# Loading the first q and k in halves of consecutive rows, with a new queue order, in an attention and MLP-mixer kernel

## The chip, the cores and the metric

The kernel runs on one core of one Trainium2 chip. The time of a run is the device time of that core in microseconds (us). Every run is listed with the mean granted clock of TensorE; a run is in the fast state when it is within 1.5% of the fastest of the same kernel.

## The reference, cut to what matters

```python
# q, k, v: (4, 8, 768, 64) float32; n_sink = 4, window = 128
scores = q @ k.T / 8                                  # per batch and head
keep   = (key < 4) | (0 <= query - key < 128)         # four sink keys and a window
a      = softmax(where(keep, scores, -1e9))
x      = (a @ v) in (4, 768, 512)
h  = relu(x^T @ w_tok1) @ w_tok2                      # mixes the 768 rows
u  = x + h^T
out = u + relu(u @ w_ch1) @ w_ch2                     # mixes the 512 channels
```

## The kernel before

The kernel works in eight groups of four heads. Two groups make a batch; after them TensorE runs the token products and then the channel products of that batch. Each operation is an object with its dependencies, and a small scheduler in the program orders them before anything is emitted; a list `FIRST` fixes the order of the start by hand. The first stage of a group is: load q and k, cast to bf16, transpose on VectorE in 32x32 blocks, scores.

```python
GH, Q = 4, 32                      # heads of a group; partitions of one head
PIECES = (2, 1, 1, 1, 1, 1, 1, 1)  # parts in which q and k of a group are loaded
...
C = PIECES[g]; R = S // Q // C     # S = 768: 24 rows of every partition, 12 in a half
for n, (w, c) in enumerate([(w, c) for c in range(C) for w in "qk"]):
    # partition (h, i) holds rows 24*i to 24*i + 23 of head h; part c is 12 of every 24 rows
    src = heads(q if w == "q" else k, g).rearrange("h (i r) d -> (h i) r d", i=Q)[:, ts(c, R)]
    ...
    nc.sync.dma_start(out=raws[w][:, ts(c, R)], in_=src)
...
# the transpose of part c fills 12 of every 24 columns of qT or kT
nc.vector.transpose(G.T[w].rearrange("p s x -> p (s x)").bitcast(UINT32)
                    .rearrange("p (i r) -> p r i", i=Q)[:, r], G.bf[w][:, r].bitcast(UINT32))
...
deps = G.dt["q"] + G.dt["k"]       # a score tile needs all transposes of its group
```

So a score tile of 128 consecutive keys needs both halves. A load of group 0 is one instruction for 128 partitions with 3072 contiguous bytes each, 393,216 bytes. The weights of the token products are issued by GpSimd's queue after v of group 0 has landed.

The softmax here doesn't subtract the row's maximum and nothing guards it: scores larger than these inputs give would overflow.

## Time and profile before

| | before |
|---|---|
| median of 3 runs, us | 216.26 (216.06 to 216.56) |
| span of the profiled run, us | 215.0 |
| mean granted clock of TensorE | 1.00 |
| TensorE busy | 204.2 us, 95% |
| first score matmuls | 10.42 us |
| first channel matmuls, in the chain | 31.30 us |

The prediction below shows the chain and the page. The view of busy time by stretch: the stretch, its length, the busy time of the five engines with the number of instructions, the granted clock, the busy share of the 16 DMA engines, and the GB/s that they moved.

```profile
core 0: us, PE busy (x) PEld busy (x) DVE busy (x) ACT busy (x) POOL busy (x), PEclk, DMA share, GB/s
5.00:10.00 5.00, 4.80 (x23) 1.96 (x20) 3.83 (x4) 2.66 (x4) 3.53 (x9) 1.00 0.98 355
15.00:20.00 5.00, 5.00 (x78) 2.86 (x74) 4.67 (x10) 4.49 (x6) 3.11 (x4) 1.00 1.11 173
```

The timeline (start, length, engine, line, operation, output and input, and in brackets how long the engine had been idle and what ended it): the casts of the two first halves.

```profile
4.29 0.84 ACT L235 ACTIVATE qb<-raw_q 128x768 bf16<-128x768 f32 x1 [0.16 <-DMA raw_q<-in_q_dram]
5.22 0.84 ACT L235 ACTIVATE kb<-raw_k 128x768 bf16<-128x768 f32 x1
```

### The profile page before, as it was taken

How to read it: one execution, taken by the hardware profiler on the slowest of the kernel's cores; microseconds unless marked ns; L12 is line 12 of the kernel's file. 1: busy time of each engine (PE TensorE's matmuls, PEld its weight loads, DVE VectorE, ACT ScalarE, POOL GpSimd, SP SyncE). 2: the span in 40 equal slices, each digit the busy share in tenths (PEclk: the TensorE clock that was granted, in tenths of full speed). 3: DMA queues.
4: the chain of work that ended last, by engine and by line, in shares of the span. 5: the costliest groups of instructions: out<-in, count | busy, mean ns of one | idle time of the engine just before them, and what ended most of it. 6: DMA issues, size and time to landing. Idle time of an engine off the chain costs nothing.

```text
span 215.0 us, 4175 instructions
## 1 busy us (share of the span) xinstructions
PE 204.2 (95%) x1764; PEld 115.8 (54%) x1764; DVE 128.2 (60%) x224; ACT 108.3 (50%) x178; POOL 33.3 (15%) x54
## 2 busy tenths in 40 slices
PE   7899999999689999979999999999999999999993
PEld 2336766554246655556655544667555545655552
DVE  4778941689899999988998912787531122001121
ACT  8489456534837233989627520696453302743300
POOL 7648810002262200211000000000000000000000
PEclk9999999999999999999999999999999999999999
DMA  6999999999999993860001012200001122001122
GB/s 193 366 226 169 204 198 203 206 208 233 219 223 236 250 196 85 161 110 0 3 0 49 3 49 107 92 0 3 0 3 49 49 97 98 3 2 49 49 98 101
DMA packets 36244, 24.68 MB, mean 115 GB/s; under 512 B 26112, under 2 KB 30976, under 8 KB 36224
## 3 DMA queue, kind: packets, MB, share of 16 engines
q1 hardware_dynamic: 29184, 15.73, 28.9%
q0 software_dynamic: 7040, 8.67, 24.1%
q8 instruction: 14, 0.23, 0.4%
q14 instruction: 6, 0.05, 0.1%
HBM read 26.77 MB, written 6.29 MB: 154 GB/s over the span
## 4 chain that ended last, share of the span: by engine, by line
PE 85%; DVE 7%; ACT 3%; DMA 3%; issue 1%; SPq 0%; ACTq 0%
PE ps_w L687 29%; PE ps_v L665 28%; PE ps_s L455 6%; PE ps_h L580 5%; PE ps_u L632 5%; DVE pT L483 4%; PE ps_o L531 3%; DMA raw_q<-in_q_dram 3%; PE ps_o L528 2%; PE ps_o L536 2%; PE ps_ut L642 2%; ACT pT L472 2%; DVE x_b L552 1%; PE ps_s L448 1%; PE ps_k L509 1%
## 5 line engine op out<-in xcount | busy, mean ns | idle before, releaser
L665 PE MATMUL ps_v<-uT,w_ch 128*128 128x384 bf16 x384 | 67.9, 326 | 0.0
L239 ACT ACTIVATE v<-ps_v 128x384 bf16<-128x384 f32 x89 | 43.5, 493 | 48.5 <-PE ps_v L665 37.3
L687 PE MATMUL ps_w<-w_ch,v 128*128 128x512 bf16 (+1 forms) x300 | 66.1, 371 | 0.0
L472 ACT ACTIVATE pT<-ps_s 128x1024 bf16<-128x1024 f32 (+1 forms) x48 | 43.7, 954 | 13.8 <-PE ps_s L455 9.4
L665 PEld LDWEIGHTS <-w_ch 128*128 128x128 bf16 x384 | 36.5, 98 | 25.3 <-DVE x_b L552 0.4
L697 DVE TENSOR_TENSOR o<-ps_w,u_sb 128x512 f32<-128x512 f32 (+1 forms) x25 | 16.7, 669 | 55.8 <-PE ps_w L687 55.8
L687 PEld LDWEIGHTS <-v 128*128 128x128 bf16 x300 | 28.9, 98 | 29.6 <-issue 0.2
L483 DVE TENSOR_TENSOR pT<-pT,mrest 128x1536 bf16<-128x1536 bf16 (+2 forms) x21 | 23.1, 1098 | 1.5 <-ACT pT L472 1.5
L637 DVE TENSOR_TENSOR u_sb<-ps_u,x_b 128x512 bf16<-128x512 f32 x24 | 15.2, 684 | 10.1 <-PE ps_u L632 10.1
L552 DVE TENSOR_TENSOR x_b<-ps_o,rc 128x256 bf16<-128x256 f32 (+1 forms) x45 | 19.9, 442 | 1.6
L455 PE MATMUL ps_s<-qT,kT 32*128 32x256 bf16 (+1 forms) x384 | 18.2, 264 | 1.6 <-ACT pT L472 1.0
L403 DVE STREAM_TRANSPOSE qT<-qb 128x768 uint32<-128x768 uint32 (+1 forms) x9 | 16.8, 1869 | 4.1 <-ACT qb L235 1.8
L531 PE MATMUL ps_o<-va,pT 128*128 128x65 bf16 x192 | 16.3, 194 | 1.7 <-DVE o L697 1.4
L403 DVE STREAM_TRANSPOSE kT<-kb 128x768 uint32<-128x768 uint32 (+1 forms) x9 | 16.9, 1874 | 0.4 <-POOL kb L234 0.4
L234 POOL CAST va<-raw_v 128x1536 bf16<-128x1536 f32 x7 | 10.5, 1493 | 42.2 <-DMA raw_v<-in_v_dram 27.2
L455 PEld LDWEIGHTS <-kT 32*128 32x128 bf16 x384 | 9.8, 92 | 11.9 <-issue 8.3
L531 PEld LDWEIGHTS <-pT 128*128 128x128 bf16 x192 | 13.4, 98 | 3.7 <-DVE o L697 1.7
L536 PE MATMUL ps_o<-va,pT 128*128 128x65 bf16 x160 | 14.8, 193 | 0.0
L632 PE MATMUL ps_u<-h,w_tok 128*128 128x512 bf16 x48 | 12.6, 378 | 0.6 <-ACT uT L235 0.5
L580 PE MATMUL ps_h<-x_b,w_tok 128*128 128x256 bf16 x96 | 12.2, 273 | 0.0
L536 PEld LDWEIGHTS <-pT 128*128 128x128 bf16 x160 | 11.3, 98 | 0.8 <-issue 0.3
L235 ACT ACTIVATE uT<-ps_ut 128x512 bf16<-128x512 bf16 (+1 forms) x14 | 7.8, 566 | 7.5 <-PE ps_ut L642 7.3
(63 smaller groups left out, 135.8 us busy)
## 6 DMA issues: line engine op xcount, KB each, us to landing
out_dram<-o SPq DMA_DIRECT2D x23, 256.0 KB, 2.0
raw_v<-in_v_dram SPq DMA_DIRECT2D x7, 768.0 KB, 12.3
qb<-in_q_dram POOLq DMA_DIRECT2D x6, 384.0 KB, 8.3
kb<-in_k_dram POOLq DMA_DIRECT2D x6, 384.0 KB, 12.2
w_ch<-in_moe_w_ch_dram POOLq DMA_DIRECT2D x4, 384.0 KB, 9.5
w_ch<-in_moe_w_ch_dram POOLq DMA_DIRECT2D x1, 1024.0 KB, 15.2
raw_q<-in_q_dram SPq DMA_DIRECT2D x2, 384.0 KB, 4.5
raw_k<-in_k_dram SPq DMA_DIRECT2D x2, 384.0 KB, 5.1
```

The source lines that it names most:

```text
L239: nc.scalar.activation(o, i, AF.Relu)
L403: nc.vector.transpose(G.T[w].rearrange("p s x -> p (s x)").bitcast(UINT32).rearrange("p (i r) -> p r i", i=Q)[:, r], G.bf[w][:, r].bitcast ...
L455: nc.tensor.matmul(bank[h][:, at:at + w], G.T["k"][r, ts(kt, P), db], G.T["q"][r, ds(kt * P, w), db], start=not pem and db == 0, stop=db = ...
L472: nc.scalar.activation(o, i, AF.Exp, scale=scale)
L483: nc.vector.tensor_tensor(out=t, in0=t, op=ALU.mult, in1=m[:, 0:hi - lo].rearrange("p (o x) -> p o x", o=1).to_broadcast([P, GH, hi - lo]))
L531: nc.tensor.matmul(ps[:, h], G.pT[qt // 2][:, h, ds(256 * (qt % 2), P)], G.va[:, h, qt], start=(qt < 2 and h == 0), stop=(h == GH - 1 and ...
L536: nc.tensor.matmul(ps[:, h], G.pT[kt // 2][:, h, ds(256 * (kt % 2) + P, P)], G.va[:, h, kt], start=False, stop=(h == GH - 1), skip_group_c ...
L552: nc.vector.tensor_tensor(out=xb.tile[:, ds(q0, n), c0:c0 + W].rearrange("p n (h d) -> p n h d", h=GH), in0=ps[:, :, :, 0:D], in1=rc.to_br ...
L580: nc.tensor.matmul(p.tile, w_tok1[:, t, ts(tt, P)], xb.tile[:, t, ds(a * W, W)], start=(t == 0), stop=(t == NT - 1))
L632: nc.tensor.matmul(ps, w_tok2[:, tt, ts(st, P)], M.h1t[:, tt], start=(tt == 0), stop=(tt == NTOK - 1))
L665: nc.tensor.matmul(ps, w_ch1[:, c, ts(ft, P)], M.uT[hf][:, c], start=(c == 0), stop=(c == NC - 1))
L687: nc.tensor.matmul(p.tile, M.v1t[hf][:, ft, ts(st % NH, P)], w_ch2[:, ft, ds(lo, n)], start=(ft == 0), stop=(ft == NF - 1))
```

## The change

The intent: rows 0 to 383 of q and k are loaded first, as half of the sequence rather than half of every partition's rows. Key tiles 0 and 1 need only those rows, so the scores can begin when the first halves are there. The order of loads and the whole `FIRST` list were searched anew for this, q and k of group 1 are loaded in halves too, and the first channel matmuls come in two parts of two so that they can start on half of their input.

```diff
-PEM = ((0, 0), (0, 1), (1, 2))
-PIECES = (2, 1, 1, 1, 1, 1, 1, 1)
+PEM = ((0, 0), (0, 1), (0, 2), (1, 2))
+PIECES = (2, 2, 1, 1, 1, 1, 1, 1)
...
-            src = heads(q if w == "q" else k, g).rearrange("h (i r) d -> (h i) r d", i=Q)[:, ts(c, R)]
+            src = heads(q if w == "q" else k, g)[:, ts(c, S // C)].rearrange("h (i r) d -> h i (r d)", i=Q)
...
-                    G.T[w].rearrange("p s x -> p (s x)").bitcast(UINT32).rearrange("p (i r) -> p r i", i=Q)[:, r],
-                    G.bf[w][:, r].bitcast(UINT32))
+                    G.T[w][:, ts(c, S // C)].rearrange("p s x -> p (s x)").bitcast(UINT32).rearrange("p (i r) -> p r i", i=Q),
+                    G.bf[w][:, ts(c, S // Q // C)].bitcast(UINT32))
...
-            deps = G.dt["q"] + G.dt["k"]
+            deps = [o for w, end in (("k", 2 * u + 2), ("q", min(2 * u + 3, NT))) for o in G.dt[w][:-(-end * C // NT)]]
...
+            for lo, hi in ((0, NC // 2), (NC // 2, NC)) if b == hf == 0 and ft < 4 else ((0, NC),):
... (the FIRST list is replaced whole; the rule that kept the loads of groups 0 and 1 in one order is dropped)
```

## The prediction

> **What bounds the kernel now.** I read the page first (busy shares, the 40 slices), then the chain in order of time, then the timeline of the first 32 us engine by engine, then the waits of GpSimd and of the DMA queue, and last the busy time by stretch.
>
> ```profile
> PE 204.2 (95%) x1764; PEld 115.8 (54%) x1764; DVE 128.2 (60%) x224; ACT 108.3 (50%) x178; POOL 33.3 (15%) x54
> ...
> 1.26 8.54 PE L800 MATMUL ps_warm<-warm 128*128 128x512 bf16 x32 [1.26 <-DVE warm L255]
> ...
> 7.38 0.84 ACT L235 ACTIVATE qb<-raw_q 128x768 bf16<-128x768 f32 x1 [1.31 <-DMA raw_q<-in_q_dram]
> 8.25 1.13 DVE L403 STREAM_TRANSPOSE qT<-qb 128x384 uint32<-128x384 uint32 x1 [1.01 <-ACT qb L235]
> 8.35 0.84 ACT L235 ACTIVATE kb<-raw_k 128x768 bf16<-128x768 f32 x1
> 9.23 1.13 DVE L403 STREAM_TRANSPOSE kT<-kb 128x384 uint32<-128x384 uint32 x1
> 10.15 0.23 DVE L427 TENSOR_TENSOR kz<-kT,blk 128x32 bf16<-128x32 bf16 x1
> ...
> 10.42 0.51 PE L455 MATMUL ps_s<-qT,kT 32*128 32x256 bf16 x8 [0.61 <-DVE kz L427]
> ...
> 10.97 0.81 ACT L472 ACTIVATE pT<-ps_s 128x768 bf16<-128x768 f32 x1 [1.77 <-PE ps_s L455]
> ...
> 12.07 5.18 ACT L472 ACTIVATE pT<-ps_s 128x1024 bf16<-128x1024 f32 x5 [0.29 <-PE ps_s L455]
> ...
> 16.63 0.96 DVE L233 CAST va<-raw_v 128x1536 bf16<-128x1536 f32 x1 [0.22 <-DMA raw_v<-in_v_dram]
> ...
> 16.89 1.83 POOL L745 DMA_DIRECT2D w_tok<-in_moe_w_tok_dram  x2 [2.60 <-DMA raw_v<-in_v_dram]
> ```
>
> The first line says that TensorE is busy 95% of the span; from the first score matmul at 10.42 us on it is the bound nearly everywhere. Before that it only runs 32 filler matmuls. What sets 10.42 is a load chain: second half of q lands at 7.36, cast, transpose, second half of k, cast, transpose, sink keys, scores. The first halves were there long before (q cast at 4.29, k cast at 5.22), but a half is 12 of every 24 rows, so it serves no score tile alone. From 10.97 ScalarE is the co-bound: twelve exponentials and two of the sink scores, almost without a gap, until
>
> ```profile
> 23.04 0.84 ACT L472 ACTIVATE pT<-ps_s 128x768 bf16<-128x768 f32 x1
> ...
> 31.30 7.80 PE ps_v L665 x48
> ...
> 54.00:56.00 2.00, 1.37 (x20) 0.59 (x18) 1.31 (x3) 1.81 (x4) 0.32 (x1) 1.00 1.33 223
> 56.00:58.00 2.00, 1.10 (x6) 0.38 (x4) 2.00 (x2) 2.00 (x3) 1.26 (x1) 1.00 1.26 213
> 58.00:60.00 2.00, 1.38 (x30) 1.02 (x31) 1.97 (x5) 0.51 (x2) 0.68 (x1) 1.00 1.34 222
> ```
>
> The first line is the last exponential of group 1 (end 23.88), the second the first channel matmuls in the chain (their records start at 31.14), the last three the only long stretch where TensorE is not full: about 2.2 us idle in these three windows (PE is the second number), with VectorE full and the DMA at its limit.
>
> **What the Trainium skill says.** "ScalarE: Activation LUTs", section "What ACT_TABLE_LOAD costs": an ACTIVATE with immediates takes 186 ns plus 0.833 ns an element, and successive ones overlap by about 93 ns. That gives 1.04 us for 1024 elements and 0.83 for 768; the trace has 1.03 and 0.82 for the exponentials, 0.84 for the casts: it agrees. "DMA: Bandwidth & Descriptors", section "Queues, rings and completion order": an engine consumes the descriptors of one ring in ring order and shares itself between queues by packets. The trace agrees in that the loads of SyncE's queue land in the order of issue (3.5 us after issue for the first q, 4.0 for the first k). So moving a load forward in that queue delays what it passes. "GPSIMD Engine Reference", section "1. Specifications": GpSimd and VectorE share SBUF interfaces. In the trace the same 128x1024 mask takes 0.68 us alone and 1.95 beside a GpSimd cast. "TensorE: Matmul & The Clock Gate", section "Part 1: The HAM clock gate": full clock comes with some 3.4 us of activity and goes after as long an idle window. The trace's granted clock is 1.00 throughout, and 19 fillers still give over 5 us, so I expect no cold matmuls after the start.
>
> **The change part by part.** (1) Halves are now rows 0 to 383 and 384 to 767 (3072 contiguous bytes per partition, as before), for both groups; the scores of key tiles 0 and 1 need only the first halves of k and q, the sink keys only the first half of k. (2) The order of loads is k, q, q, k for group 0, then k, q, q of group 1, then v of group 0, then the last k half, then v of group 1. (3) Three casts move from ScalarE and GpSimd to VectorE, so ScalarE, which had four half casts, now has two before the exponentials and one among them. (4) The mask of tile pair 2 of group 0 goes from one VectorE multiply (0.95 us) to four 128x384 matmuls (4 x 0.16 = 0.65 us of TensorE). (5) 19 fillers instead of 32: 13 x 0.216 = 2.8 us shorter, ending near 9.80 - 2.8 = 7.0. (6) Two token-mixing row tiles (4 matmuls x 0.216 = 0.86 us) no longer precede the first channel matmul; channel matmuls in two parts fill that place instead.
>
> Early schedule, with the old landings taken by position in the queue (4.25, 5.2, 7.36, 8.3). k cast on VectorE, half of the 0.96 us row plus overhead, 0.55: 4.80. Transpose 1.13: 5.93. Sink keys 0.2: 6.15. q cast on ScalarE ends 6.05; transpose 6.15 to 7.3. First scores at about 7.35, against 10.42: 3.1 us earlier. But ScalarE's list has the second k cast ahead of the first exponential: it waits for the fourth landing, 8.3, and ends at 9.2. So the first exponential starts near 9.2 against 10.97, 1.8 us earlier, and the third score pair, which needs the second k transpose, cannot start before 10.3.
>
> From there ScalarE: before, 12.91 us from the first to the last exponential, of which 0.77 idle, so 12.14 of work. After: 12.14 + 0.84 for one q cast among them = 13.0, if it never waits. Last exponential ends at 9.2 + 13.0 = 22.2 against 23.88. One stall looks likely: TensorE's list puts the first value products, which need v of group 0, before four of the six score pairs of group 1. v landed at 16.55; one half (393 KB, about 1.1 us at the 366 GB/s of the page's second slice) is taken from in front of it, so about 15.5, cast to 16.5, perhaps 17.0 if the engines share. TensorE would come to it near 16, so 0.5 to 1.0 us of stall, part of which ScalarE feels. I take the last exponential at 22.2 to 23.0, and the last scores 1.0 us earlier (22.87 against 23.88 before): 21.3 to 22.0.
>
> From the last scores to the first channel matmul was 31.14 - 22.87 = 8.27 us of nearly gapless TensorE. It loses the 0.86 us of (6) and one value product (9 matmuls, 0.36) which now comes earlier: 7.05. So channel matmuls at 28.4 to 29.1. The moved 0.86 is paid later, so the comparison is with 31.14 - 0.86 = 30.28: gain 1.2 to 1.9 us, 1.5 in the middle.
>
> After that TensorE runs the same work, but the lists differ. In the 54 to 64 us stretch the new list puts four-matmul pieces of the second channel product between the score and value pieces of group 2, which fills idle time; the VectorE list there is more crowded in return. I give this 0.3 us of gain, an estimate with plus or minus 1 us. Sum: 1.5 + 0.3 = 1.8; 216.26 - 1.8 = 214.5.
>
> **The rivals.** (a) *A transfer takes the place of the wait.* The first token weight is issued only after v lands (the 2.60 us GpSimd wait), needs 5.2 to 6.0 us to land, so came between 22.1 and 22.9, just before its first use at 22.87. If it does not move forward, TensorE gains nothing before 22.9, the last scores apart. For: DMA busy over 1.0 in nearly every window. Against: v is one place earlier, and at 18 to 20 us the DMA share was only 0.75, a hole that an earlier issue fills. The q load of group 2 (first transpose waits until 43.75) is the same question; old TensorE reached those scores at 52.54, the new one near 51, the transposes are done at 50.2: enough. If this rival holds, 215.5 to 216.5. (b) *The whole 3.1 us carries over.* For: TensorE is the bound later. Against: ScalarE's first exponential gains 1.8 and its list is 0.84 longer. It would give 213.2. (c) *The middle stretch decides.* There VectorE masks ran beside GpSimd casts and took 1.95 and 2.51 us instead of 0.68 and 1.23. If the new times keep casts and masks apart, up to 2.5 us more comes out: 212.0. If they meet worse, the gain is gone: 215.8.
>
> **Range and chances.** The centre is 214.5. The early part is good for 1.0 to 2.0, the middle for -1.0 to +1.5; together 213.0 to 215.9. A gain of 2% needs 211.9, thus almost all of (b) or all of (c) on top: 5%. A loss of 2% would need 4.3 us lost in later lists that hold the same work: 1%. Within 2%: 94%.
>
> **What would show each step.** First scores at 7.2 to 7.6 us and first exponential at 9.0 to 9.5, waiting on a k cast or its DMA. Score matmuls of pair 1 at 10.3 behind the transpose. ScalarE nearly full from 9.2 to 22 or 23. A wait of 0.5 to 1.0 us before the first value product, ended by VectorE's v cast. First channel matmul at 28.4 to 29.1, with 12 row-tile matmuls after it rather than 8. I am wrong in kind if the channel matmuls start after 30.3 (weights late), if the first scores come after 8.5, or if the chain past 54 us loses more than the early part won.

## More of the kernel before

The runs of one call go to one chip together with runs of the kernel before.

## The result, and the profile after

| | before | after |
|---|---|---|
| median, us | 216.25 (4 runs, 216.06 to 216.56) | 249.16 (4 runs, 248.39 to 249.77) |
| span of the profiled run, us | 215.0 | 246.3 |
| mean granted clock | 1.00 | 0.90 |
| first score matmuls, us | 10.42 | 14.17 |
| first channel matmuls, in the chain, us | 31.30 | 62.44 |
| from there to the end, us | 183.7 | 183.9 |

The changed kernel is 15% slower: the ratio is 1.152, 95% interval 1.148 to 1.155. Here and below a ratio is the mean time of one kernel's runs over that of the other's runs of the same rounds, so it is not quite the ratio of the medians.

The last two rows of the table say where to look. The first channel matmuls come 31.1 us later, and the span is 31.3 us longer: the loss lies before them. What follows takes as long as before, although two row tiles (four matmuls, 0.86 us) were moved behind that point; like for like the later part is 0.7 us shorter.

The same view by stretch, of the kernel after (columns as above):

```profile
5.00:10.00 5.00, 3.61 (x13) 1.37 (x12) 1.59 (x3) 0.00 (x0) 4.08 (x9) 1.00 0.33 97
10.00:15.00 5.00, 0.83 (x8) 0.47 (x7) 0.90 (x2) 0.84 (x1) 0.00 (x0) 0.85 0.27 100
15.00:20.00 5.00, 3.15 (x14) 0.91 (x13) 1.41 (x2) 0.00 (x0) 0.00 (x0) 0.50 0.26 103
40.00:60.00 20.00, 12.71 (x131) 8.39 (x130) 9.71 (x24) 5.08 (x6) 6.62 (x9) 0.55 0.98 149
60.00:80.00 20.00, 19.86 (x130) 11.61 (x130) 12.08 (x17) 9.30 (x19) 0.00 (x0) 1.00 1.15 206
```

Read the last two columns first. From 5 to 20 us the DMA engines are a quarter to a third busy and move about 100 GB/s, where from 5 to 10 us they were full and moved 355. A quarter of 16 is four. 103 / 4 = 25.8 GB/s for each busy engine, and before it was 399 / 16 = 24.9 in the stretch from 8 to 10 us: a busy engine is as fast as ever. The share is a mean over all 16; that it is four engines at work all the time, and not 16 for a quarter of it, is shown below under theory E. Then read the clock, the third number from the right: it falls to 0.50, since TensorE has little to do, and is back at 1.00 from 60 us on.

The timeline of the kernel after shows what the four engines do to the start:

```profile
8.34 0.60 DVE L234 CAST kb<-raw_k 128x768 bf16<-128x768 f32 x1 [4.46 <-DMA raw_k<-in_k_dram]
...
12.40 0.84 ACT L236 ACTIVATE qb<-raw_q 128x768 bf16<-128x768 f32 x1 [8.27 <-DMA raw_q<-in_q_dram]
...
14.17 1.04 PE L455 MATMUL ps_s<-qT,kT 32*128 32x256 bf16 x8 [5.57 <-DVE qT L403]
...
20.02 0.84 ACT L236 ACTIVATE kb<-raw_k 128x768 bf16<-128x768 f32 x1 [6.78 <-DMA raw_k<-in_k_dram]
20.77 1.92 ACT L472 ACTIVATE pT<-ps_s 128x1024 bf16<-128x1024 f32 x2
...
36.58 1.83 POOL L748 DMA_DIRECT2D w_tok<-in_moe_w_tok_dram  x2 [10.16 <-DMA raw_v<-in_v_dram]
```

The halves land one by one, at about 8.3, 12.4, 16.1 and 20.0 us, against four in 4.1 us before. The distance is that of 393,216 bytes at 103 GB/s, 3.8 us. The first scores still start on two halves, as intended, but the second of these landed at 12.4 us, and before, all four had landed by 8.3. The last line is the same delay further on: the token weights are issued at 36.58, before at 16.89, because v of group 0 waits its turn.

The chain of waits of the kernel after (start, length, what) says so in another way:

```profile
4.51 4.21 SPq L360
8.76 3.85 SPq L360
12.66 3.65 SPq L360
16.36 3.62 SPq L382
20.02 14.11 SPq L360
34.73 18.67 DMA raw_v<-in_v_dram
53.53 1.48 POOL va L235
...
62.44 7.89 PE ps_v L668 x48
```

Up to 34 us the chain is SyncE's queue, not an engine that computes. An issue took 0.37 to 0.45 us in the kernel before for these loads. Here the fifth issue ends at 8.72, just after the first half has landed, the sixth at 12.61 after the second, the seventh at 16.31 and the eighth, v of group 0, at 19.98 after the third and the fourth: with four half loads in flight the queue takes the next one only when one has landed. The 14.11 us are the second half of k of group 1. With v among the loads in flight that issue ended only after three more halves had landed, so the limit is not simply a count of loads. The last v half then needs 18.67 us; by now the weights, which are issued when v of group 0 lands, are in flight beside it.

### The profile page after: what moved, and what is told of

Read it like the earlier page. It is cut to its first block, busy times and chain, and to the rows that moved or that the text cites. A ratio compares the mean times of both kernels' runs of the same rounds, so it can differ in the third digit from the quotient of the medians.

```text
span 246.3 us, 4139 instructions
## 1 busy us (share of the span) xinstructions
PE 213.3 (87%) x1734; PEld 119.5 (49%) x1755; DVE 128.3 (52%) x235; ACT 104.5 (42%) x171; POOL 31.5 (13%) x53
## 4 chain that ended last, share of the span: by engine, by line
PE 72%; SPq 14%; DMA 8%; DVE 3%; issue 1%; ACT 1%; POOL 1%; POOLq 0%
PE ps_v L668 26%; PE ps_w L690 25%; SPq L360 12%; DMA raw_v<-in_v_dram 8%; PE ps_h L580 4%; PE ps_u L632 4%; PE ps_s L455 4%; PE ps_ut L642 2%; PE ps_o L531 2%; PE ps_o L536 2%; SPq L382 2%; PE ps_o L528 2%; DVE pT L483 1%; ACT pT L472 1%; POOL va L235 1%
## 5 line engine op out<-in xcount | busy, mean ns | idle before, releaser
L668 PE MATMUL ps_v<-uT,w_ch 128*128 128x384 bf16 x384 | 69.4, 329 | 0.5 <-PE ps_o L536 0.3
L690 PE MATMUL ps_w<-w_ch,v 128*128 128x512 bf16 (+1 forms) x288 | 65.0, 370 | 0.8 <-issue 0.3
L240 ACT ACTIVATE v<-ps_v 128x384 bf16<-128x384 f32 x84 | 40.9, 494 | 49.2 <-PE ps_v L668 38.3
L455 PE MATMUL ps_s<-qT,kT 32*128 32x256 bf16 (+1 forms) x384 | 21.8, 294 | 10.1 <-DVE qT L403 5.6
L531 PE MATMUL ps_o<-va,pT 128*128 128x65 bf16 x192 | 18.3, 207 | 3.7 <-POOL va L235 3.2
L531 PEld LDWEIGHTS <-pT 128*128 128x128 bf16 x192 | 15.7, 106 | 7.2 <-issue 5.2
L483 DVE TENSOR_TENSOR pT<-pT,mrest 128x1024 bf16<-128x1024 bf16 (+2 forms) x20 | 18.8, 950 | 0.4 <-ACT pT L472 0.2
L403 DVE STREAM_TRANSPOSE qT<-qb 128x768 uint32<-128x768 uint32 (+1 forms) x10 | 15.5, 1585 | 3.3 <-ACT qb L236 3.2
L536 PE MATMUL ps_o<-va,pT 128*128 128x65 bf16 x160 | 16.8, 206 | 0.0
L536 PEld LDWEIGHTS <-pT 128*128 128x128 bf16 x160 | 13.2, 108 | 1.2 <-issue 0.4
L448 PE MATMUL ps_s<-mneg,ident 128*128 128x384 bf16 (+1 forms) x15 | 6.5, 528 | 8.3 <-ACT pT L472 8.3
L551 DVE RECIPROCAL rc<-ps_o 128x4 f32<-128x4 f32 (+1 forms) x45 | 8.0, 177 | 9.2 <-PE ps_o L536 7.8
```

Source lines behind the costliest of these rows:

```text
L240: nc.scalar.activation(o, i, AF.Relu)
L403: nc.vector.transpose(G.T[w][:, ts(c, S // C)].rearrange("p s x -> p (s x)").bitcast(UINT32).rearrange("p (i r) -> p r i", i=Q), G.bf[w][: ...
L455: nc.tensor.matmul(bank[h][:, at:at + w], G.T["k"][r, ts(kt, P), db], G.T["q"][r, ds(kt * P, w), db], start=not pem and db == 0, stop=db = ...
L483: nc.vector.tensor_tensor(out=t, in0=t, op=ALU.mult, in1=m[:, 0:hi - lo].rearrange("p (o x) -> p o x", o=1).to_broadcast([P, GH, hi - lo]))
L531: nc.tensor.matmul(ps[:, h], G.pT[qt // 2][:, h, ds(256 * (qt % 2), P)], G.va[:, h, qt], start=(qt < 2 and h == 0), stop=(h == GH - 1 and ...
L536: nc.tensor.matmul(ps[:, h], G.pT[kt // 2][:, h, ds(256 * (kt % 2) + P, P)], G.va[:, h, kt], start=False, stop=(h == GH - 1), skip_group_c ...
```

## The experiments

**Theory E.** The loss is the number of DMA engines that a half load uses. The Trainium skill, "DMA: Bandwidth & Descriptors", section "Why a DMA increments its semaphore by 16 and not by 1", says that the descriptor generator takes the slowest dimension of more than one element of each side of the copy and spreads the transfer over the largest number of engines, 16 at most, that divides both sizes. Work it out from the code. Before, a partition's rows are 24 x 64 = 1536 elements apart, and 32 x 1536 = 49,152 is the distance of two heads: heads and row blocks merge into one dimension of 128, so 16 engines. After, the blocks are 12 x 64 = 768 apart, and 32 x 768 = 24,576 is half of that distance: the dimensions can't merge, and the slowest of the source is the 4 heads, so 4 engines. The trace agrees, with 103 GB/s and a share of 0.26.

The kept traces also show the engines themselves, in the single packets and semaphore updates that the views here sum up (a DMA tells of its landing by updates of a semaphore, a counter). Apart from one update right after the issue, the first half of k in the kernel after is told by four, between 7.48 and 8.32 us; a half in the kernel before is told by 16, and a load of experiment 2 by two. And from 13 to 16 us, four packets are in progress in the kernel after at 91% of all moments; in the kernel before it was 16 or 17 at 98%, from 8 to 10 us.

**Rivals.** The new order of instructions could itself be the loss (more halves, other casts); the half clock could be the cause rather than a consequence (rival C); and, for the repair by small loads, the time that issues take could bound it (rival I). Nine kernels were run; all gave the right result.

**1. Each half as four loads of one head** (e1). Then the slowest source dimension is the 32 blocks of a head, which 16 divides.

```diff
-                    nc.sync.dma_start(out=raws[w][:, ts(c, R)], in_=src)
+                    for h in range(GH):
+                        nc.sync.dma_start(out=raws[w][ds(Q*h, Q), ts(c, R)], in_=src[h])
```

> The changed kernel with each half load of q and k issued as four loads of one head (32 partitions) each; everything else as it is. Theory E (engines): in the changed kernel a half load's source has the 4 heads as its slowest dimension and so runs on 4 of the 16 DMA engines, 103 GB/s; one head's 32 rows go over 16 again. Then the DMA windows from 5 to 12 us show near 300 GB/s, the halves land within about 2 to 3 us of each other's issue, and the time falls from 249 to between 213 and 221 us (the four-fold issues of about 0.43 us each cost a few us early). Theory O (order of the queue, v ahead of the last k half): the queue order is the same, so the time stays above 240. Theory L (reading consecutive halves is slow in itself, whatever the engines): the rate stays near 100 GB/s and the time near 249.

Measured: 220.70 us (219.97 to 221.09), ratio to before 1.021 (1.017 to 1.024). 28 of the 33 us are gone with the same bytes in the same order. The window of this kernel, and its cast of v of group 0:

```profile
10.00:15.00 5.00, 3.31 (x26) 1.56 (x26) 2.08 (x4) 3.64 (x5) 0.82 (x1) 0.93 0.75 212
```

```profile
20.16 0.96 DVE L234 CAST va<-raw_v 128x1536 bf16<-128x1536 f32 x1 [2.21 <-DMA raw_v<-in_v_dram]
```

The rate doubles to 212 GB/s but does not reach the 300 expected. One issue takes 0.46 us, and 98,304 bytes in 0.46 us are 214 GB/s: SyncE can't feed more. The first 28 loads all landed 2.1 to 2.8 us after their issues, the 28th after 2.4, so no backlog grew. With the rate, the rest of the intent comes out. The first scores start at 8.06 and the first exponential at 11.25. But v is cast at 20.16, before at 16.63, since SyncE comes to it at 13.81, and the channel matmuls start at 34.78. The granted clock was 0.50 from 15 to 20 us and 0.77 from 20 to 30, so part of what is still lost here may be the clock; in experiments 5 and 6 it was 1.00 in these stretches.

**2. Each half as two loads of two heads** (e2), which theory E puts on two engines.

```diff
+                    for h in (0, 2):
+                        nc.sync.dma_start(out=raws[w][ds(Q * h, 2 * Q), ts(c, R)], in_=src[h:h + 2])
```

> The changed kernel with each half load issued as two loads of two heads (slowest dimension 2). The dose test. Theory E: two engines, so half the rate again: about 50 GB/s in the first 50 us, a DMA share near 0.13, each half landing about 7.5 us after the one before, and the time 25 to 35 us above 249. Theory O: as the changed kernel, about 249. Theory L: as the changed kernel or a little better.

Measured: 279.21 us, one look, 30 us more than the kernel after.

```profile
15.00:20.00 5.00, 0.00 (x0) 0.00 (x0) 0.00 (x0) 0.33 (x1) 0.00 (x0) 0.50 0.13 52
```

The share is 0.13, two of sixteen, at 52 GB/s, and the halves land 7.7 us apart. More loads of the same bytes made it worse here and better in experiment 1, so it is not the number of loads, but the heads in each.

**3. The kernel before, with only group 0's halves as consecutive rows** (e3). The order of TensorE is that of before.

```diff
-            src = heads(q if w == "q" else k, g).rearrange("h (i r) d -> (h i) r d", i=Q)[:, ts(c, R)]
+            src = heads(q if w == "q" else k, g)[:, ts(c, S // C)].rearrange("h (i r) d -> h i (r d)", i=Q)
```

(and the transpose as in the change).

> The kernel before, with only the layout of the four half loads of group 0 changed to consecutive rows (and the transposes' output with it); order, casts, fillers and what the scores wait for as before. Theory E: these four loads run at 103 GB/s, so the fourth lands at about 16 to 17 us in place of 8.35, the first scores start 8 us later, and the time is 223 to 228 us. Theory O: 216, since the order is the old one. Theory L: as E (it does not tell E from L; the two runs with single heads and pairs do).

Measured: 238.06 us, one look. The layout of four loads alone costs 22 us, without the new order. The size is 10 us beyond what was expected, and the timeline says why:

```profile
8.23 0.84 ACT L235 ACTIVATE qb<-raw_q 128x768 bf16<-128x768 f32 x1 [4.10 <-DMA raw_q<-in_q_dram]
...
14.24 0.84 ACT L235 ACTIVATE kb<-raw_k 128x768 bf16<-128x768 f32 x1 [5.17 <-DMA raw_k<-in_k_dram]
```

The halves are 6 us apart, not 3.8. The packets of this trace say more, since a half moves in packets of 3072 bytes and a whole-partition load of group 1 in packets of 6144. From 10 to 14 us, four half packets are in progress at 92% of all moments, as in the kernel after, and beside them mostly twelve of group 1: the loads behind did not take over the four engines. But the median half packet took 226 ns, where from 5 to 8 us it took 124. So the later halves were not overtaken; they were slowed while other engines worked beside them. Why a packet then takes longer, the runs do not show.

**4. The changed kernel with the old interleaved layout** (e4): the new list, the halves of group 1, the fewer fillers and the two-part matmuls stay; the layout and the dependencies that go with it are those of before.

```diff
-            src = heads(q if w == "q" else k, g)[:, ts(c, S // C)].rearrange("h (i r) d -> h i (r d)", i=Q)
+            src = heads(q if w == "q" else k, g).rearrange("h (i r) d -> (h i) r d", i=Q)[:, ts(c, R)]
...
-            deps = [o for w, end in (("k", 2 * u + 2), ("q", min(2 * u + 3, NT))) for o in G.dt[w][:-(-end * C // NT)]]
+            deps = G.dt["q"] + G.dt["k"]
```

> The changed kernel with the old layout of the halves (12 of every 24 rows, 128 as the slowest dimension), so that the scores wait for both halves again; queue order, list of instructions, mask of pair 2 on TensorE and channel matmuls in two parts stay. Theory E: loads at full rate, time 214 to 220. Theory O: still above 235. Theory L: 214 to 220 as E.

Measured: 215.03 us (214.49 to 215.42), ratio 0.995 (0.993 to 0.998), clock 1.00. That settles the first rival: the new order loses nothing, and with full-rate loads it is half a percent faster than the kernel before (the interval excludes 1; the difference is small). Where that comes from, in the windows of this kernel and then of the kernel before:

```profile
5.00:10.00 5.00, 5.00 (x24) 2.25 (x23) 4.42 (x5) 1.69 (x2) 4.62 (x10) 1.00 0.95 332
...
50.00:60.00 10.00, 8.76 (x113) 4.68 (x115) 8.81 (x14) 7.62 (x12) 4.96 (x3) 1.00 1.26 222
60.00:70.00 10.00, 10.00 (x135) 6.20 (x128) 9.37 (x21) 6.10 (x8) 3.65 (x6) 1.00 1.15 231
```

```profile
50.00:60.00 10.00, 7.85 (x88) 3.89 (x86) 8.73 (x11) 5.54 (x8) 3.73 (x3) 1.00 1.26 220
60.00:70.00 10.00, 8.93 (x123) 5.35 (x121) 9.49 (x19) 5.54 (x8) 4.32 (x6) 1.00 1.19 232
```

The DMA is at 332 GB/s again. The gain is not at the start: its first score matmuls come at 10.75, and the channel matmuls at 31.22, with 0.86 us of row tiles moved behind them, so 0.8 us later like for like. From 50 to 70 us TensorE is busy 18.76 us, before 16.78: 2.0 us less idle in the middle stretch. What brought it the runs do not separate; one of VectorE's masks there took 1.22 us (at 57.57), where before it took 2.51 us beside a cast (at 59.35).

**5 and 6. Rows per head for group 0 only, group 1 in halves of the old layout, on one queue (e5), and with the first half of q issued by ScalarE (e6).** This halves the number of small loads, from 32 to 16.

```diff
+                    if g == 0:
+                        for h in range(GH):
+                            nc.sync.dma_start(out=raws[w][ds(Q * h, Q), ts(c, R)], in_=src[h])
+                    else:
+                        nc.sync.dma_start(out=raws[w][:, ts(c, R)], in_=src)
... e6 in addition: the first half of q by ScalarE's queue, and a fill of 128x2080 from ScalarE to VectorE
```

> The intent at full load rate: group 0 in halves of consecutive rows, each as four loads of one head (16 engines each), so that its scores may begin on the first half; group 1 in halves of the old layout with one load each; all other parts of the change kept. SyncE issues 16 + 4 loads of q and k instead of 32. Theory E alone: first scores at about 8 us (as with single heads in both groups), v of group 0 issued at about 10 us instead of 13.8 and landing about 17, no cold clock of long duration, time 213 to 217. Rival I (issue-bound): the 16 issues of 0.46 us on SyncE still hold back k and q of group 1 and v, and the time is 217 to 220, worse than the old layout with the same lists (215.0).

> As the run before it, with the four loads of the first half of q issued by ScalarE and the sink-value memset moved from ScalarE to VectorE to make room: 12 + 4 loads on SyncE. Both theories: first scores near 7 to 7.5 us. Theory E alone: 212.5 to 216. Rival I: about 1 to 2 us better than the run before, since four issues (1.8 us) leave SyncE's queue.

Measured: e5 221.88 us (219.86 to 222.06), ratio 1.023 (1.016 to 1.029); e6 221.11 us (220.81 to 221.98), ratio 1.023 (1.019 to 1.027). Both are worse than both theories expected, and the second queue gains nothing that can be told from noise: the medians differ by 0.8 us, the ratios are both 1.023. The first scores are at 9.27 and 8.96, earlier than the 10.42 of before, but this does not carry over. In e5's timeline:

```profile
9.64 0.44 SPq L390 DMA_DIRECT2D raw_v<-in_v_dram  x1
...
18.18 1.83 POOL L758 DMA_DIRECT2D w_tok<-in_moe_w_tok_dram  x2 [5.21 <-DMA raw_v<-in_v_dram]
```

v of group 0 is issued at 9.64 us (before at 3.61), the token weights at 18.18, 1.3 us later than before (16.89), and the channel matmuls start at 34.31, 3.0 us later. That is not all: from there to the end e5 takes 186.1 us, before 183.7, and its chain now waits 9.88 us for v and 7.45 us for q of later groups (at 50.64 and 62.08), where the chain before has no such wait. What is late at the start is passed on to later loads.

**7. The half loads of the kernel after on GpSimd's queue** (e7). The skill's section named above says that this queue picks its four engines in turn instead of always the same.

```diff
-                    nc.sync.dma_start(out=raws[w][:, ts(c, R)], in_=src)
+                    nc.gpsimd.dma_start(out=raws[w][:, ts(c, R)], in_=src)
```

> The changed kernel with the eight half loads issued by GpSimd instead of SyncE, nothing else changed. The source still has 4 heads as slowest dimension. If a load of that shape takes the same four engines on this queue too, the rate stays near 100 GB/s and the time is 240 to 260. If, as the skill's DMA page says for this path, it takes four engines in turn, four loads in flight cover all 16 engines: over 250 GB/s from 4 to 12 us, all halves landed by 14 us, time 216 to 226.

Measured: 235.06 us, one look, between the two expectations. The loads of v, now alone on SyncE, started at 0.8 us and ran beside the halves: the share was above 1.0, at 136 to 179 GB/s from 5 to 15 us. The run moved more than the one thing it was to test. Its packets still decide on the engines: of GpSimd's queue, 8 or 9 packets of 6144 bytes were in progress from 6 to 9 us at 99% of all moments, and 14 to 17 from 11 to 13 us. So these loads together used more than four engines, which agrees with that section. But such a packet took 0.48 us from 11 to 13 us (median), in the kernel before 0.23 us from 8 to 10 us, and the first cast came at 15.43. Why the packets were so slow is not shown.

**8. The kernel after with filler matmuls** (e8), to hold the clock: twelve before each of the first twelve score pieces, 24 before the first token product.

```diff
+                if g < 2:
+                    for _ in range(12):
+                        nc.tensor.matmul(bank[hs[0]], warm[:, 0:P], warm, start=True, stop=True, skip_group_check=True)
```

> The changed kernel with its loads as they are, and 12 more filler matmuls ahead of each of the twelve score pieces of groups 0 and 1 and 24 short ones ahead of the first token product, so that TensorE's clock stays full through the waits. Theory E: the half-speed clock between 13 and 57 us is a consequence, not the cause; v of group 1 still lands at 53 to 54 us, and the time is 245 to 250 (at most 3 us better). Rival C (the clock costs the time): 230 to 240. Granted clock in the 15 to 55 us windows should go from 0.50 to near 1 for the run to count.

Measured: 257.75 us, one look, clock 0.987.

```profile
20.00:30.00 10.00, 8.27 (x50) 3.66 (x50) 1.94 (x3) 3.33 (x4) 0.82 (x1) 1.00 0.71 145
```

```profile
53.91 1.47 POOL L235 CAST va<-raw_v 128x1536 bf16<-128x1536 f32 x1 [13.72 <-DMA raw_v<-in_v_dram]
```

The clock is 1.00 where it was 0.50, and the loads land where they did: the casts of the halves are at 8.25, 12.27, 16.11 and 19.96, that of v of group 1 at 53.91 (53.53 in the kernel after). So the late loads do not come from the clock. My size was off by 8 us: from 31 us on the fillers stand in TensorE's own way, so the total does not say what the half clock costs by itself. The chain of the kernel after gives a bound. Up to 53.53 us it holds only queue and DMA; from the last v cast to the channel matmuls, 55.0 to 62.4 us, TensorE ran at a mean clock of 0.81. At full clock these 7.4 us would be 6.0 (an estimate), so rival C is worth about 1.4 us of the 33 there, and falls as the cause.

**9. e5 with v of group 0 issued first, by ScalarE's queue** (e9), to test rival I where it was left open: is it v's late issue that makes e5 slow?

```diff
-            G.load["v"].append(op(f"Lv{g}.{x}", ("SP", 0.46), vv, vdeps, ...
+            G.load["v"].append(op(f"Lv{g}.{x}", {"SP": 0.46, "ACT": 0.46} if g == 0 else ("SP", 0.46), vv, vdeps, ...
... in the list of the start: Lv0.0 first of all, on ScalarE
```

> The kernel of e5 (group 0's halves as consecutive rows, one load per head; group 1 in the old interleaved layout) with one more change: v of group 0 is issued first of all by ScalarE's queue instead of after the sixteen head loads and three others on SyncE's. Theory I (e5 and e6 lose because sixteen issues of 0.46 us put v and with it the token weights late): v is issued near 1 us instead of 9.64 and lands before 12 us instead of 17.6; the first token weight is issued before 13 us instead of 18.18; the first channel matmul in the chain comes before 32.5 us instead of 34.3; time 213 to 219 us, 3 us or more better than e5. Rival B (the bytes ahead of the scores decide): v's 786 KB share the engines with the first halves, the first scores come after 10.5 us instead of 9.27, and what v gains the scores lose: 220 to 224 us. The lists past the first scores shift too, so a difference under 1.5 us would tell nothing.

Measured: 238.71 us (238.13 to 241.48), ratio 1.107 (1.099 to 1.116). In its timeline:

```profile
8.80 0.62 DVE L234 CAST kb<-raw_k 128x768 bf16<-128x768 f32 x1 [4.91 <-DMA raw_k<-in_k_dram]
...
9.54 2.01 POOL L758 DMA_DIRECT2D w_tok<-in_moe_w_tok_dram  x2
```

and in its chain:

```profile
16.76 20.74 DMA raw_v<-in_v_dram
```

The first step of theory I held, and more: the token weights are issued at 9.54. The rest fell. The first half of k lands at 8.8 instead of 4.4 us, the first scores start at 12.76, and the weights, now early, are in flight beside v of group 1, which the chain waits 20.74 us for. Rival B was right in kind (v takes from the first halves) and far too small, as it had nothing on v of group 1. What a queue gains for one transfer, the others pay.

## Why the prediction was wrong

**The step that failed** is the sentence "Early schedule, with the old landings taken by position in the queue (4.25, 5.2, 7.36, 8.3)", and under it that a half has "3072 contiguous bytes per partition, as before". The bytes per partition are indeed the same; the way in which the dimension of heads is carried is not. The landings were about 8.3, 12.4, 16.1 and 20.0. Experiments 1, 2 and 4 show it from three sides: the same rows at one head per load, two heads per load, and the old layout under the new order. All that follows in the prediction hangs on those four numbers:

- First scores at 7.35: they came at 14.17. From the landing of the first half of q to the scores the prediction allowed 2.15 us; it was 1.8 in the kernel after and 1.9 in experiment 1, so the working behind the step was sound. The k cast took 0.60 (0.55 assumed), the half transpose 0.85 (1.13 assumed). The fillers ended at 8.17, not near 7.0.
- First exponential at 9.2, waiting on the second k cast: 20.77, waiting on exactly that cast. The last exponential of group 1, put at 22.2 to 23.0, ended at 51.7.
- Stall of 0.5 to 1.0 us before the first value products: v landed at 36.29, not at 15.5.
- First channel matmul at 28.4 to 29.1: 62.44 in the chain. This was named as the sign of being wrong in kind (after 30.3, weights late).
- 0.3 us of gain in the later lists: 0.7 us like for like, and with full-rate loads 2.0 us less idle on TensorE from 50 to 70 us. The place was right, and the size is within the plus or minus 1 us in the first case only; that the pieces of the channel product did it is not shown (experiment 4). The reading of the lines was also short: TensorE is idle 3.2 us from 54 to 64 us, not 2.2 us in three windows only, and VectorE is not full in the first of them (1.31 of 2 us).
- "I expect no cold matmuls after the start": wrong. The granted clock was 0.50 from 15 to 50 us. It follows from the late data, and cost little by itself (experiment 8).

**The rivals.** (a) named the right kind, a transfer in the place of the wait, and gave it at most 2 us over its centre: it looked at weights and at q of group 2, not at the loads that the diff itself edits. (b) was never reached. (c) can be read in experiment 4 alone, where one of the two slow masks became fast and the other still took 1.95 us beside a cast. The chance of 1% for a loss of over 2% came from counting work in the later lists; nothing there was wrong, and it was the wrong place.

**What stays open.** Whether the early start itself would pay is not shown. No kernel here loaded halves of consecutive rows at the full rate without many small issues: e1, e5 and e6 start scores 1.1 to 2.4 us earlier than before and still lose 2%, with v and weights late, and e9 shows that moving v first is no cure. The 22 us of experiment 3 are shown, but not why a packet takes longer while other engines work, nor why the packets of experiment 7 were slow.

## What to carry to other kernels

When a diff changes the access pattern of a load, work out whether its outermost dimensions still merge on both sides before you take over any landing time, even if bytes, partitions and contiguous runs are the same: here a slice that broke one merge cut the rate to a quarter. The sign in a profile is a DMA share near k/16 with the issuing queue in the chain. When small loads are the repair, count issue time times their number, since 0.46 us an issue was the next bound, and ask which transfer is pushed back by the one that you move forward.

## What the Trainium skill lacked or had wrong

- "DMA: Bandwidth & Descriptors", section "Why a DMA increments its semaphore by 16 and not by 1": its rule held (a slowest dimension of 4 gave a share of 0.26 and 103 GB/s, of 2 gave 0.13 and 52 GB/s; the packets show four and two at a time), and section "Rules for kernel authors" warns of an outermost dimension under 16, with a broadcast as its example; that slicing rows below a head dimension breaks a merge, and what it cost here (15% of this kernel's time), is not there.
- The same page, section "Issuing engines are not separate DMA queues": it calls issue time usually small beside the transfer. Here 0.46 us for each load of 98,304 bytes capped the rate at 212 GB/s where the engines moved 355.
- The same page, section "Queues, rings and completion order": I found nothing there on how many loads a queue holds. With four half loads on four engines in flight, the fifth issue lasted until the first landed, and the longest, with v in flight as well, took 14.11 us.
- The same page: I found nothing there on how much a packet slows while other engines work. In experiment 3 a packet of 3072 bytes took 226 ns beside twelve packets of other engines and 124 ns without them, and the second half landed 6 us after the first, not 3.8, though no later load overtook it.
- "VectorE: DVE Perf Modes", section "The three transpose paths": I found no word on the output's layout. The same 128x384 transpose took 1.13 us with the interleaved output and 0.85 us with a contiguous half.
